# Two handoffs between layers: the last rows' statistics earlier, the last row's moments on ScalarE, row copies in one-bank tiles with guess products between them, small clears on GpSimd

## The chip, the cores and the metric

One core of one Trainium2 chip. The metric is the device time of one execution in microseconds. An execution's clock is the mean granted TensorE clock of its core, 1.000 being full speed. The ratios and their intervals are those of the record, from the fast runs of the same rounds; they are not quite the ratios of the medians that are quoted beside them, nor of the plain means (clears_only: 1586.44 over 1586.81 us is 0.9998, the record has 1.0000).

## The reference, cut to what matters

```python
x = x + A(layernorm(x))      # A: irfft2(rfft2(x) * W), 2048 tokens x 640
x = x + B(layernorm(x))      # B: attention by segments of 32 with 8 memory rows, 32 heads of 128
x = x + A(layernorm(x))
x = x + B(layernorm(x))
```

Layer B's memory goes from one segment to the next, so the kernel first guesses all memories and then repairs the guess. The first guess is made from sums over each segment ("u", made from the tile "psu") and Wv; its products are "psvb". The result of the last layer norm of A is what B starts from: u, and the transposed tokens "hT". The stretch in which A ends and B begins is called the handoff here. There are two, near 107 and 885 us.

## The kernel before

A works through 16 tiles ("rows") of 128 tokens. Row i's eviction, its moments, the inverse deviation of a pair of rows and the scaling ("norm") are spread over ScalarE, VectorE and GpSimd. This is the loop and what follows it (cut):

```python
for i in range(16 + 1):
    ...
    if i >= 5 and i % 2 == 1:
        norm((i - 5) // 2)              # VectorE, then a store
    if i >= 2:
        stats(i - 2)                    # VectorE: two BATCH_NORM_STATS2, one AGGREGATE
    ...
    if 1 <= i <= 16:
        tokens(i - 1)                   # ScalarE evicts the row: the "last token tile" is row 15
    ...
    if i >= 4 and i % 2 == 0:
        inverse((i - 4) // 2, nc.gpsimd)   # ScalarE: log and exponential; GpSimd: the scale
    ...
stats(15)
norm(6)
for s0 in range(14):
    handoff.add_u(pp, xna[:, s0, :], s0)   # TensorE: segment sums of one row, 5 products
big = handoff.big(pp)                      # one tile over two PSUM banks
inverse(7, nc.vector)
...
norm(7)
for s0 in (14, 15):
    handoff.add_u(pp, xna[:, s0, :], s0)
handoff.finish(pp)                         # ScalarE: u <- psu
...
pairs = [handoff.rows_in(pp, xna, 3, 2 * n, ps=big[:, 2 * n:2 * n + 2]) for n in range(2)]   # transposes
ones = [handoff.rows_in(pp, xna, q, 4) for q in (2, 3)]
for job, on_dve in ((pairs[0], True), (pairs[1], False), (ones[0], True), (ones[1], True)):
    handoff.do(handoff.rows_out(job, on_dve))     # row copies by VectorE or ScalarE
handoff.guess1(pp)                                # 160 products, four ScalarE evictions
```

The small clears at the start of layer B stand in VectorE's queue:

```python
nc.vector.memset(sums_sb[:, GQ:], 1.0)
for KT in KTs:
    for a, b in ((502, 512), (1007, 1024), (1519, 1536), (2035, 2048)):
        nc.vector.memset(KT[:, a:b], 0.0)
```

Of the kernel before, what the change touches and what calls it, by code (L numbers as in the profile page):

```python
# [10 lines left out]
FP32 = mybir.dt.float32  # L11
BF16 = mybir.dt.bfloat16
I32 = mybir.dt.int32
ALU = mybir.AluOpType
ACTF = mybir.ActivationFunctionType
# [4 lines left out]
S, D = 2048, 640  # L20
# [81 lines left out]
def _ln_stats(nc, st, mv, x_row, t):  # L102
    for hlf in range(2):
        nc.vector.bn_stats(out=st[:, t % 2, hlf, :], in_=x_row[:, hlf * 320:(hlf + 1) * 320])
    nc.vector.bn_aggr(out=mv[:, t, :], in_=st[:, t % 2, :, :])
# [86 lines left out]
class LayerA:  # L192
# [330 lines left out]
    def tokens(self, x_dst, xn_dst, handoff=None):  # L523
        tc, g, UT, Gd, Ti, x = self.tc, self.g, self.UT, self.Gd, self.Ti, self.x
        nc = tc.nc
        xd, xnd = r16(x_dst), r16(xn_dst)
        s5 = self.ar.get("S5", f"{self.lname}tok")
        Gs = [s5.bf(2, NF) for _ in range(3)]
        xna = s5.bf(16, D)
        wk, st, mv = g["ln"], {}, {}  # L530
        halves = lambda ap: ap.rearrange("p (a b) -> p a b", a=2)
        pp = self.pp
# [29 lines left out]
        def stats(s0):  # L562
            _ln_stats(nc, st[s0 // 2], mv[s0 // 2], x[:, s0, :], s0 % 2)

        def inverse(q, small):
            rs[q], _ = _ln_inverse(nc, wk, mv[q], 2, g["eps"], small)

        def norm(q):
            xno = xna[:, 2 * q:2 * q + 2, :]
            _ln_scale(nc, mv[q], rs[q], x[:, 2 * q:2 * q + 2, :], xno, 2)  # L570
            nc.sync.dma_start(out=xnd[:, 2 * q:2 * q + 2, :], in_=xno)

        with tc.manual_schedule(engines={nc.tensor.engine, nc.scalar.engine, nc.vector.engine}):
            moved, late = [], []
            for i in range(16 + 1):
                for f in moved:
                    f()
                moved = []
                if late:
                    late.pop(0)()  # L580
                if i >= 5 and i % 2 == 1:
                    norm((i - 5) // 2)
                if i >= 2:
                    stats(i - 2)
                if i < 16:
                    spectrum_d(i)
                if 1 <= i <= 16:
                    tokens(i - 1)
                for f in late:
                    f()  # L590
                late = []
                if i >= 4 and i % 2 == 0:
                    inverse((i - 4) // 2, nc.gpsimd)
                if handoff is None:
                    continue
                if i < 10:
                    handoff.wv_piece(i)
                if i == 5:
                    handoff.memory(pp)
                if i >= 8 and i % 4 < 3:  # L600
                    n = i % 4
                    jobs = handoff.rows_out(handoff.rows_in(pp, xna, i // 4 - 2, 2 * n), n != 1 and i < 16)
                    if n == 1:
                        late = jobs
                    else:
                        moved = jobs
            stats(15)
            norm(6)
            if handoff is not None:
                for s0 in range(14):  # L610
                    handoff.add_u(pp, xna[:, s0, :], s0)
                big = handoff.big(pp)
            inverse(7, nc.vector)
            if handoff is not None:
                handoff.do(moved)
                second = handoff.rows_in(pp, xna, 2, 2)
            norm(7)
            if handoff is not None:
                for s0 in (14, 15):
                    handoff.add_u(pp, xna[:, s0, :], s0)  # L620
                handoff.finish(pp)
                handoff.do(handoff.rows_out(second, False))
                pairs = [handoff.rows_in(pp, xna, 3, 2 * n, ps=big[:, 2 * n:2 * n + 2]) for n in range(2)]
                ones = [handoff.rows_in(pp, xna, q, 4) for q in (2, 3)]
                for job, on_dve in ((pairs[0], True), (pairs[1], False), (ones[0], True), (ones[1], True)):
                    handoff.do(handoff.rows_out(job, on_dve))
                handoff.guess1(pp)
        pp.release()


H, DH, MEM, SEG, NSEG = 32, 128, 8, 32, 64
# [37 lines left out]
class _Stream:  # L669
# [15 lines left out]
    GQ = GS * SW  # L685
# [330 lines left out]
def _b_fast_pass(tc, g, bs, env, flag_col, nxt=None):  # L1016
    nc = tc.nc
    st = bs.st
    hT, gq, oTm = bs.hT, bs.gq, bs.oTm
    ones = g["ones"]  # L1020
    oTx_d = g["oTx_d"]
    PRE, SW, GS, NG, NT, NQ, QPRE = st.PRE, st.SW, st.GS, st.NG, st.NT, st.NQ, st.QPRE
    scale = float(DH) ** -0.5
# [6 lines left out]
    last = {}  # L1030
    ar = env["ar"]
    GQ, NL = st.GQ, NQ - st.GQ * (NG - 1)
# [5 lines left out]
    accR, accS = s3.f32(GQ + NL), s3.f32(GQ + NL)  # L1038
# [5 lines left out]
    Es = [s5.bf(512) for _ in range(2)]  # L1044
    Rb1, sums_sb = s5.f32(NQ), s5.f32(GQ + NL)
    Rs = [s4.f32(GQ + NL), g["R"][:]]
    for t in (accR, accS):
        nc.gpsimd.memset(t, 0.0)
    if True:
        nc.vector.memset(sums_sb[:, GQ:], 1.0)  # L1050
        for KT in KTs:
            for a, b in ((502, 512), (1007, 1024), (1519, 1536), (2035, 2048)):
                nc.vector.memset(KT[:, a:b], 0.0)
        Vt = {}

        def load_w(hp):
# [110 lines left out]

        def sums_ln(h):
            nc.scalar.activation(out=Rs[h % 2], in_=sums_sb, func=ACTF.Ln, bias=g["floor"][:, 0:1])
            nc.gpsimd.tensor_tensor(out=accS, in0=accS, in1=sums_sb, op=ALU.add)  # L1170
            if 0 < h < H - 1:
                sums_acc(h - 1)

        def sums_acc(h):
            nc.gpsimd.tensor_tensor(out=accR, in0=accR, in1=Rs[h % 2], op=ALU.add)

        def sums_back(h):
            R = Rs[h % 2]
# [52 lines left out]
        out = _FastOut(tc, g, env, nxt)  # L1231
# [15 lines left out]
        bufs, blocks = [s3.at(0, HL, 256), s6.at(0, HL, 256)], {}  # L1247
# [9 lines left out]
        if True:  # L1257
            for h in range(H + 2):
# [35 lines left out]
                elif h == H:  # L1294
# [5 lines left out]
                    x = ar.get("S4", f"b{bs.lname}x").bf(16, D)  # L1300
# [26 lines left out]
    with octx:  # L1327
# [17 lines left out]
        n = [0]  # L1345
# [61 lines left out]
class BStart:  # L1407
# [35 lines left out]
        nc.vector.tensor_copy(out=self.hT[:, :, 0:MEM], in_=psm[:, :, 0:MEM])  # L1443
        nc.vector.tensor_copy(out=self.gq[:, :, 0:1], in_=psm[:, :, MEM - 1:MEM])

    def guess1(self, pp):
        nc = self.tc.nc
        self.s6 = self.ar.get("S6", f"b{self.lname}")
        self.vb = self.s6.at(2 * 3 * 5 * 256, H, NSEG)
        for q in range(4):  # L1450
            ps = pp.tile([128, 2, 512], FP32, name="psvb", tag="pg", bufs=3)[:, 0, :]
            for h8 in range(8):
                h = 8 * q + h8
                for c in range(5):
                    nc.tensor.matmul(ps[:, h8 * NSEG:(h8 + 1) * NSEG], lhsT=self.Wv_sb[:, c, h * 128:(h + 1) * 128], rhs=self.u[:, c, :],  # L1455
                                     start=(c == 0), stop=(c == 4))
            nc.scalar.copy(out=self.vb[:, 8 * q:8 * q + 8, :].rearrange("p a b -> p (a b)"), in_=ps)

    def big(self, pp):
        return pp.tile([128, 4, 4, 128], BF16, name="pstrb", tag="pg", bufs=3)  # L1460

    def do(self, jobs):
        for f in jobs:
# [223 lines left out]
```

## Time and profile before

| before | value | how to read it |
|---|---|---|
| time | 1587.33 us median of 3 (1586.22 to 1587.96) | one core |
| profiled execution | 1583.7 us, clock 0.998 | the trace is of one execution, not of the median one |
| last token tile to u | 6.56 us in both handoffs | start of ScalarE's eviction of row 15 to start of u |
| u to first psq | 9.00 us in handoff 1, 7.76 us in handoff 2 | row copies and guess products |

The lines of the views are in the prediction below. A timeline line gives start and length in us, engine, line of the source and operation, and in brackets the idle time before it and who ended it. Lines of the changed kernel have other numbers for the same code: L1053 became L1074, L1085 L1106, L1433 L1460, L1457 L1490, L1507 L1540.

### The profile page before, as it was taken

What the parts mean: (1) busy time and instruction counts of PE and PEld (TensorE: products, weight loads), DVE (VectorE), ACT (ScalarE), POOL (GpSimd) and SP (SyncE); (2) the same over time, 40 slices, a digit from 0 to 9 for tenths busy, and PEclk for the clock granted to TensorE, in tenths of its full rate; (3) what the DMA queues carried; (4) which work ended last, traced back from release to release, by engine and by line L of the source; (5) the groups of instructions that cost most, each with busy time, mean ns of one, the idle gap of its engine ahead of it and who ended that gap; (6) DMA issues with size and microseconds to landing.
All of it is one profiled execution on the core that took longest, in us unless ns stands there. A gap on an engine that the chain in (4) does not pass through costs nothing.

```text
span 1583.7 us, 36625 instructions
## 1 busy us (share of the span) xinstructions
PE 1542.4 (97%) x14420; PEld 1073.2 (68%) x14421; DVE 786.1 (50%) x2220; ACT 831.9 (53%) x2541; POOL 283.3 (18%) x311
## 2 busy tenths in 40 slices
PE   6989999999999999999999899999999999999998
PEld 5666666666666667677766666666766666667775
DVE  7872545555454554543377535555454545554101
ACT  4474666666666666511126656666666666663000
POOL 3620111121111212100034111121211112120000
PEclk9999999999999999999999999999999999999999
DMA  4680445535444463646114514435454454537242
GB/s 167 213 301 8 122 138 139 153 111 167 135 135 139 118 176 97 209 104 184 51 49 148 187 53 120 151 114 172 131 140 130 122 173 126 145 96 226 67 127 64
DMA packets 159922, 214.13 MB, mean 135 GB/s; under 512 B 7230, under 2 KB 133500, under 8 KB 151804
## 3 DMA queue, kind: packets, MB, share of 16 engines
q1 hardware_dynamic: 159132, 209.41, 44.5%
q8 instruction: 114, 1.87, 0.5%
q0 software_dynamic: 608, 2.30, 0.4%
q14 instruction: 68, 0.56, 0.1%
HBM read 166.59 MB, written 45.09 MB: 134 GB/s over the span
## 4 chain that ended last, share of the span: by engine, by line
PE 89%; DVE 4%; POOL 3%; issue 2%; ACT 1%; DMA 1%; SPq 0%; DVEq 0%; POOLq 0%; ACTq 0%
PE psv L1132 19%; PE psk L1066 18%; PE psx L1366 18%; PE psq L1066 17%; PE pso L1201 5%; PE pss L1142 4%; PE psl L1160 2%; PE psg L541 1%; PE psq L1085 1%; PE psm L840 1%; PE psg L1519 1%; DVE A1tmp_S L456 1%; DVE A2tmp_S L456 1%; PE psvb L1455 0%; DMA A1x_S<-in_A_x_dram 0%
## 5 line engine op out<-in xcount | busy, mean ns | idle before, releaser
L1066 PEld LDWEIGHTS <-bB_S 128*128 128x128 bf16 x3180 | 258.1, 97 | 174.7 <-issue 1.1
L1210 DVE TENSOR_TENSOR bB_S<-pso,bB_S 128x480 bf16<-128x480 f32 (+1 forms) x320 | 189.6, 593 | 246.7 <-PE pso L1201 235.6
L1145 ACT ACTIVATE bB_S<-pss 128x269 bf16<-128x269 f32 (+5 forms) x576 | 203.9, 386 | 199.2 <-PE pss L1142 194.0
L1366 PE MATMUL psx<-Wo_sb,bB_S 128*128 128x320 bf16 x2048 | 287.7, 299 | 0.0
L1125 DVE CAST bB_S<-psk 128x495 bf16<-128x495 f32 (+3 forms) x320 | 191.8, 600 | 114.1 <-PE psk L1066 75.8
L1366 PEld LDWEIGHTS <-bB_S 128*128 128x128 bf16 x2048 | 197.1, 98 | 74.3 <-DVE bB_S L1210 0.7
L1146 DVE TENSOR_TENSOR bB_S<-bB_S,maskf 128x269 bf16<-128x269 bf16 (+5 forms) x576 | 159.5, 289 | 162.1 <-ACT bB_S L1145 162.1
L1170 POOL TENSOR_TENSOR bB_S<-bB_S,bB_S 128x634 f32<-128x634 f32 x64 | 97.9, 1530 | 770.3 <-ACT bB_S L1166 770.3
L1134 ACT CAST bB_S<-psv 128x512 bf16<-128x512 f32 (+1 forms) x288 | 161.1, 560 | 75.7 <-PE psv L1132 75.0
L1110 ACT ACTIVATE bB_S<-psq 128x96 bf16<-128x96 f32 x300 | 152.4, 508 | 91.3 <-PE psq L1066 90.4
L1132 PE MATMUL psv<-bB_S,B1hT_S 128*128 128x256 bf16 x1360 | 166.2, 273 | 0.0
L1132 PE MATMUL psv<-bB_S,B2hT_S 128*128 128x256 bf16 x1360 | 166.2, 273 | 0.0
L1066 PE MATMUL psk<-B1hT_S,bB_S 128*128 128x495 bf16 (+3 forms) x800 | 162.5, 343 | 0.4 <-ACT bB_S L1087 0.2
L1066 PE MATMUL psk<-B2hT_S,bB_S 128*128 128x495 bf16 (+3 forms) x800 | 162.5, 343 | 0.3 <-ACT bB_S L1087 0.2
L1142 PEld LDWEIGHTS <-bB_S 128*128 128x128 bf16 x1216 | 99.7, 97 | 84.4
L1066 PE MATMUL psq<-B1hT_S,bB_S 128*128 128x495 bf16 (+5 forms) x780 | 153.2, 336 | 0.0
L1066 PE MATMUL psq<-B2hT_S,bB_S 128*128 128x495 bf16 (+5 forms) x780 | 153.2, 336 | 0.0
L1132 PEld LDWEIGHTS <-B2hT_S 128*128 128x128 bf16 x1360 | 127.5, 98 | 14.6 <-issue 0.2
L1132 PEld LDWEIGHTS <-B1hT_S 128*128 128x128 bf16 x1360 | 127.5, 98 | 14.6 <-issue 0.2
L1142 PE MATMUL pss<-bB_S 128*128 128x132 bf16 (+8 forms) x1216 | 133.2, 216 | 0.1
L1201 PE MATMUL pso<-bB_S,bB_S 128*128 128x132 bf16 (+8 forms) x1216 | 120.3, 216 | 1.5 <-DVE oTmf L1211 1.4
L1201 PEld LDWEIGHTS <-bB_S 128*128 128x128 bf16 x1216 | 90.7, 98 | 22.9 <-DVE oTmf L1211 4.0
(271 smaller groups left out, 1538.5 us busy)
## 6 DMA issues: line engine op xcount, KB each, us to landing
bB_S<-Rd SPq DMA_DIRECT2D x62, 1059.5 KB
oTx_d<-bB_S SPq DMA_DIRECT2D x60, 512.0 KB
bB_S<-oTx_d SPq DMA_DIRECT2D x46, 512.0 KB
bB_S<-in_B_Wq_dram SPq DMA_DIRECT2D x32, 320.0 KB
bB_S<-in_B_Wk_dram SPq DMA_DIRECT2D x32, 320.0 KB
bB_S<-in_B_Wv_dram SPq DMA_DIRECT2D x32, 320.0 KB
Wo_sb<-in_B_Wo_dram SPq DMA_DIRECT2D x4, 1280.0 KB
B1wv_S<-in_B_Wv_dram SPq DMA_DIRECT2D x10, 512.0 KB
```

The source lines that it names most:

```text
L1066: nc.tensor.matmul(ps, lhsT=w[:, ch, hh * 128:(hh + 1) * 128], rhs=src[:, ch, lo:hi], start=(ch == 0), stop=(ch == 4))
L1110: nc.scalar.mul(out=qv[:, :, 0:SEG], in_=x_view(ps, o, n)[:, :, 1:SW], mul=scale)
L1125: nc.vector.tensor_copy(out=KTs[h % 2][:, lo:hi], in_=ps[:, 0:hi - lo])
L1132: nc.tensor.matmul(ps[:, i * 256:(i + 1) * 256], lhsT=hT[:, ch, st.hcol((t + i) * 128):st.hcol((t + i) * 128) + 128], rhs=w["Wv"][:, ch, : ...
L1134: nc.scalar.copy(out=V[:, t:t + n, :].rearrange("p a b -> p (a b)"), in_=ps[:, 0:n * 256])
L1142: nc.tensor.matmul(ps[:, off - o0:off - o0 + hi - lo], lhsT=KT[:, t * 128:(t + 1) * 128], rhs=QT[:, lo:hi], start=True, stop=True)
L1145: nc.scalar.activation(out=E[:, 0:n], in_=ps[:, 0:n], func=ACTF.Exp)
L1146: nc.vector.tensor_tensor(out=P[:, o0:o0 + n], in0=E[:, 0:n], in1=bs.mask[:, o0:o0 + n], op=ALU.mult)
L1170: nc.gpsimd.tensor_tensor(out=accS, in0=accS, in1=sums_sb, op=ALU.add)
L1201: nc.tensor.matmul(pso[:, lo - q0:hi - q0], lhsT=V[:, t, (h % 2) * 128:(h % 2 + 1) * 128], rhs=P[:, off:off + hi - lo], start=(i == 0), st ...
L1210: nc.vector.tensor_tensor(out=oT.rearrange("p (r s j) -> p r s j", r=16, j=2)[:, :, s0:s0 + ns, :], in0=byclass(po), in1=rx, op=ALU.mult)
L1366: self.tc.nc.tensor.matmul(ps[:, 0:320], lhsT=lhs(h, k // 2), rhs=self.g["Wo_sb"][:, h, c0:c0 + 320], start=(h == 0), stop=(h == H - 1))
```

## The change

It shortens the two handoffs. The moments of row 15 move to ScalarE; the moments of rows 11 to 14 go ahead of the norms; the segment sums of rows 0 to 9 go ahead of the last rows' statistics; the two-bank tile becomes two one-bank tiles; the guess products are put between the transposes in five pieces; nine small clears move to GpSimd, and two large ones become copies at the first head. The core of the diff:

```diff
+        def act_stats(s0):
...
+            nc.scalar.activation(out=scr, in_=x[:, s0, :], func=ACTF.Identity, scale=-D ** -1.5, accum_out=nm[:])
+            nc.scalar.activation(out=scr, in_=x[:, s0, :], func=ACTF.Square, scale=D ** -0.5, bias=nm[:, 0:1], accum_out=m[:, 1:2])
+            nc.gpsimd.tensor_scalar_mul(out=m[:, 0:1], in0=nm[:], scalar1=-D ** 0.5)
...
+                last = i >= 13
+                if i >= 2 and last:
+                    stats(i - 2)
                 if i >= 5 and i % 2 == 1:
                     norm((i - 5) // 2)
-                if i >= 2:
+                if i >= 2 and not last:
                     stats(i - 2)
...
+                if i == 16:
+                    for s0 in range(10):
+                        handoff.add_u(pp, xna[:, s0, :], s0)
...
-            stats(15)
+            act_stats(15)
...
-                for job, on_dve in ((pairs[0], True), (pairs[1], False), (ones[0], True), (ones[1], True)):
-                    handoff.do(handoff.rows_out(job, on_dve))
-                handoff.guess1(pp)
+                pairs = [handoff.rows_in(pp, xna, 3, 2 * n, ps=handoff.big(pp)) for n in range(2)]
+                ones = [handoff.rows_in(pp, xna, 2, 4)]
+                vb = [handoff.guess1(pp, 0)]
+                ones.append(handoff.rows_in(pp, xna, 3, 4))
+                handoff.do(handoff.rows_out(pairs[0], True))
+                handoff.do(handoff.rows_out(pairs[1], False))
+                vb.append(handoff.guess1(pp, 1))
...
-        nc.vector.memset(sums_sb[:, GQ:], 1.0)
+        nc.gpsimd.memset(sums_sb[:, GQ:], 1.0)
...
-                nc.vector.memset(KT[:, a:b], 0.0)
+                nc.gpsimd.memset(KT[:, a:b], 0.0)
...
+    GUESS = ((0, 8), (8, 16), (16, 24), (24, 28), (28, 32))
...
-        return pp.tile([128, 4, 4, 128], BF16, name="pstrb", tag="pg", bufs=3)
+        return pp.tile([128, 2, 512], FP32, name="pstrb", tag="pg", bufs=3)[:, 0, :].bitcast(BF16).rearrange("p (c i k) -> p c i k", c=2, i=4)
```

More of the change, by code (lines that the diff above doesn't have):

```diff
@@ L563, in stats @@
             _ln_stats(nc, st[s0 // 2], mv[s0 // 2], x[:, s0, :], s0 % 2)
+        def act_stats(s0):
+            m, scr = mv[s0 // 2][:, s0 % 2, :], Gs[1].rearrange("p a b -> p (a b)")[:, 0:D]
+            nm = wk.tile([128, 1], FP32, name="lnnm", tag="lnnm")
+            nc.scalar.activation(out=scr, in_=x[:, s0, :], func=ACTF.Identity, scale=-D ** -1.5, accum_out=nm[:])
+            nc.scalar.activation(out=scr, in_=x[:, s0, :], func=ACTF.Square, scale=D ** -0.5, bias=nm[:, 0:1], accum_out=m[:, 1:2])
+            nc.gpsimd.tensor_scalar_mul(out=m[:, 0:1], in0=nm[:], scalar1=-D ** 0.5)
         def inverse(q, small):
@@ L606, in tokens @@
                         moved = jobs
-            stats(15)
+            act_stats(15)
             norm(6)
-            if handoff is not None:
-                for s0 in range(14):
-                    handoff.add_u(pp, xna[:, s0, :], s0)
-                big = handoff.big(pp)
             inverse(7, nc.vector)
             if handoff is not None:
+                for s0 in range(10, 14):
+                    handoff.add_u(pp, xna[:, s0, :], s0)
                 handoff.do(moved)
@@ L622, in tokens @@
                 handoff.do(handoff.rows_out(second, False))
-                pairs = [handoff.rows_in(pp, xna, 3, 2 * n, ps=big[:, 2 * n:2 * n + 2]) for n in range(2)]
-                ones = [handoff.rows_in(pp, xna, q, 4) for q in (2, 3)]
-                for job, on_dve in ((pairs[0], True), (pairs[1], False), (ones[0], True), (ones[1], True)):
-                    handoff.do(handoff.rows_out(job, on_dve))
-                handoff.guess1(pp)
+                pairs = [handoff.rows_in(pp, xna, 3, 2 * n, ps=handoff.big(pp)) for n in range(2)]
[5 more added lines that the diff above has]
+                vb.append(handoff.guess1(pp, 1))
+                handoff.do(handoff.rows_out(ones[0], True))
+                handoff.guess1_out(0, vb[0], nc.scalar.copy)
+                vb.append(handoff.guess1(pp, 2))
+                handoff.guess1_out(1, vb[1], nc.scalar.copy)
+                handoff.do(handoff.rows_out(ones[1], True))
+                vb.append(handoff.guess1(pp, 3))
+                handoff.guess1_out(2, vb[2], nc.scalar.copy)
+                vb.append(handoff.guess1(pp, 4))
+                handoff.guess1_out(3, vb[3], nc.vector.tensor_copy)
+                handoff.guess1_out(4, vb[4], nc.scalar.copy)
         pp.release()
@@ L1046, in _b_fast_pass @@
     Rs = [s4.f32(GQ + NL), g["R"][:]]
-    for t in (accR, accS):
-        nc.gpsimd.memset(t, 0.0)
     if True:
-        nc.vector.memset(sums_sb[:, GQ:], 1.0)
+        nc.gpsimd.memset(sums_sb[:, GQ:], 1.0)
         for KT in KTs:
             for a, b in ((502, 512), (1007, 1024), (1519, 1536), (2035, 2048)):
-                nc.vector.memset(KT[:, a:b], 0.0)
+                nc.gpsimd.memset(KT[:, a:b], 0.0)
         Vt = {}
@@ L1169, in sums_ln @@
             nc.scalar.activation(out=Rs[h % 2], in_=sums_sb, func=ACTF.Ln, bias=g["floor"][:, 0:1])
-            nc.gpsimd.tensor_tensor(out=accS, in0=accS, in1=sums_sb, op=ALU.add)
+            if h:
+                nc.gpsimd.tensor_tensor(out=accS, in0=accS, in1=sums_sb, op=ALU.add)
+            else:
+                nc.gpsimd.tensor_copy(out=accS, in_=sums_sb)
             if 0 < h < H - 1:
@@ L1174, in sums_acc @@
         def sums_acc(h):
-            nc.gpsimd.tensor_tensor(out=accR, in0=accR, in1=Rs[h % 2], op=ALU.add)
+            if h:
+                nc.gpsimd.tensor_tensor(out=accR, in0=accR, in1=Rs[h % 2], op=ALU.add)
+            else:
+                nc.gpsimd.tensor_copy(out=accR, in_=Rs[0])
         def sums_back(h):
@@ L1444, in memory, with guess1, guess1_out @@
         nc.vector.tensor_copy(out=self.gq[:, :, 0:1], in_=psm[:, :, MEM - 1:MEM])
-    def guess1(self, pp):
+    GUESS = ((0, 8), (8, 16), (16, 24), (24, 28), (28, 32))
+    def guess1(self, pp, q):
         nc = self.tc.nc
-        self.s6 = self.ar.get("S6", f"b{self.lname}")
-        self.vb = self.s6.at(2 * 3 * 5 * 256, H, NSEG)
-        for q in range(4):
-            ps = pp.tile([128, 2, 512], FP32, name="psvb", tag="pg", bufs=3)[:, 0, :]
-            for h8 in range(8):
-                h = 8 * q + h8
-                for c in range(5):
-                    nc.tensor.matmul(ps[:, h8 * NSEG:(h8 + 1) * NSEG], lhsT=self.Wv_sb[:, c, h * 128:(h + 1) * 128], rhs=self.u[:, c, :],
-                                     start=(c == 0), stop=(c == 4))
-            nc.scalar.copy(out=self.vb[:, 8 * q:8 * q + 8, :].rearrange("p a b -> p (a b)"), in_=ps)
+        if q == 0:
+            self.s6 = self.ar.get("S6", f"b{self.lname}")
+            self.vb = self.s6.at(2 * 3 * 5 * 256, H, NSEG)
+        ps = pp.tile([128, 2, 512], FP32, name="psvb", tag="pg", bufs=3)[:, 0, :]
+        h0, h1 = self.GUESS[q]
+        for h in range(h0, h1):
+            for c in range(5):
+                nc.tensor.matmul(ps[:, (h - h0) * NSEG:(h - h0 + 1) * NSEG], lhsT=self.Wv_sb[:, c, h * 128:(h + 1) * 128], rhs=self.u[:, c, :],
+                                 start=(c == 0), stop=(c == 4))
+        return ps
+    def guess1_out(self, q, ps, copy):
+        h0, h1 = self.GUESS[q]
+        copy(out=self.vb[:, h0:h1, :].rearrange("p a b -> p (a b)"), in_=ps[:, 0:(h1 - h0) * NSEG])
     def big(self, pp):
-        return pp.tile([128, 4, 4, 128], BF16, name="pstrb", tag="pg", bufs=3)
+        return pp.tile([128, 2, 512], FP32, name="pstrb", tag="pg", bufs=3)[:, 0, :].bitcast(BF16).rearrange("p (c i k) -> p c i k", c=2, i=4)
     def do(self, jobs):
```

## The prediction

"They" are VectorE's and ScalarE's copies, and "that pairing" is VectorE's row copies beside GpSimd's clears, for which no effect was counted. The sum: 0.85 + 2.1 + 0.85 + 0.9 = 4.7 us, to 1582.6 us.

> **What bounds the kernel now.** I read the page first, its busy times and the chain that ended last. TensorE is busy 97% of the span and carries 89% of the chain, so a change counts only where TensorE stands still.
>
> ```profile
> PE 1542.4 (97%) x14420; PEld 1073.2 (68%) x14421; DVE 786.1 (50%) x2220; ACT 831.9 (53%) x2541; POOL 283.3 (18%) x311
> ...
> PE 89%; DVE 4%; POOL 3%; issue 2%; ACT 1%; DMA 1%; SPq 0%; DVEq 0%; POOLq 0%; ACTq 0%
> ```
>
> The change touches only the end of each layer A and its handoff to layer B, of which there are two. So next came the busy times by stretch: the two handoffs (from the last token tile to the first query matmul, "psq") and the layer-B stretches behind them. The columns are the stretch, its length, then busy time and instructions of TensorE, weight loads, VectorE, ScalarE and GpSimd, the clock and the DMA share.
>
> ```profile
> 107.00:122.50 15.50, 10.81 (x284) 9.70 (x284) 9.68 (x39) 8.87 (x21) 1.00 (x5) 1.00 0.71 214
> 885.30:899.50 14.20, 10.70 (x284) 9.70 (x285) 9.59 (x39) 8.81 (x21) 1.00 (x5) 1.00 0.76 233
> 122.50:640.00 517.50, 516.83 (x4825) 349.14 (x4825) 258.07 (x762) 322.91 (x1027) 91.84 (x60) 1.00 0.44 128
> ```
>
> The third line shows TensorE idle for 0.67 us in the 517.5 us after the first handoff: whatever moves the first psq earlier moves the end by as much. The first two show the pool to win from: 4.7 us idle in handoff 1 and 3.5 us in handoff 2, 8.2 us in all, 0.5% of the run.
>
> What is waited for there is in the table of waits of each handoff (total us, times, longest). First handoff:
>
> ```profile
> DVE bB_S L1053 <- DMA xn<-A1tok_S: 2.3, 1, 2.3
> ACT B1hT_S L1487 <- DVE B1hT_S L1494: 2.1, 1, 2.1
> ...
> PE psvb L1455 <- ACT B1hT_S L1494: 1.1, 1, 1.1
> ...
> PE pstr L1472 <- ACT B1hT_S L1491: 0.9, 1, 0.9
> ...
> PE psq L1085 <- ACT bB_S L1457: 0.7, 1, 0.7
> ```
>
> Second handoff:
>
> ```profile
> PE pstr L1472 <- ACT B2hT_S L1491: 0.9, 1, 0.9
> ...
> ACT B2hT_S L1487 <- DVE B2hT_S L1494: 0.9, 1, 0.9
> ...
> PE psq L1085 <- ACT bB_S L1457: 0.7, 1, 0.7
> ```
>
> The first handoff has a chain the second lacks. VectorE's clear of K's pad columns (L1053) waits for a store to land; the row copies behind it in VectorE's queue start at 115.70; ScalarE's copies of the other half of the same PSUM tile wait for VectorE's last one (L1494); the guess products wait for ScalarE. That is why handoff 1 takes 9.4 us from the last norm (112.3 to 113.1) to psq at 122.50, and handoff 2 only 8.2 us (norm's end 891.3, psq 899.47).
>
> Three rows of the timeline (start, length) are my anchors: the last row's moments on VectorE, the last norm, and "u", after which the guess products may run.
>
> ```profile
> 109.75 0.83 DVE L104 BATCH_NORM_STATS2 lnst<-A1x_S 128x6 f32<-128x320 bf16 x2
> ...
> 112.29 0.80 DVE L127 TENSOR_SCALAR A1tok_S<-A1x_S,lnmv,lnrs 128x640 bf16<-128x640 bf16 x2
> ...
> 113.50 0.44 ACT L1507 ACTIVATE u<-psu 128x320 bf16<-128x320 f32 x1 [0.53 <-PE psu L1433]
> ```
>
> The moments on ScalarE cost what the same two operations cost in the cold start (timeline, ScalarE):
>
> ```profile
> 4.62 0.74 ACT L283 ACTIVATE A1xn_S<-A1x_S 128x640 bf16<-128x640 bf16 x1 [2.59 <-DMA A1x_S<-in_A_x_dram]
> 5.27 0.19 ACT L283 ACTIVATION_READ_ACCUMULATOR A1xn_S<-A1x_S 128x1 f32 x1
> 5.49 0.83 ACT L284 ACTIVATE A1xn_S<-A1x_S,A1xn_S 128x640 bf16<-128x640 bf16 x1
> 6.22 0.19 ACT L284 ACTIVATION_READ_ACCUMULATOR A1xn_S<-A1x_S,A1xn_S 128x1 f32 x1
> ```
>
> From 4.62 to 6.41 is 1.79 us for a row; VectorE's own way is 1.1 us (two halves 0.83, aggregate 0.21, gaps).
>
> [...] the trace agrees that they are ordered (2.1 us and 0.9 us above), although the two halves of this tile are a bank each: the order is kept by the tile. Two one-bank tiles take it away. [...] No run so far shows that pairing. I count none.
>
> **The change part by part** (times of handoff 1; the program orders of both builds were compared, the waits taken from the built instructions).
>
> 1. Reordered statistics, last row on ScalarE. In the old order VectorE does norm(5), three rows' statistics, norm(6), then the scale of pair 7 and norm(7) at 112.29. New: VectorE is free at 106.25 (it idled 0.76 us before norm(5)), so row 13's statistics run 106.25 to 107.35, norm(5) to 108.1, row 14's to 109.2. ScalarE is free at 107.63 and takes pair 6's logarithm and exponential (0.52) to 108.2, the moments of row 15 (1.8) to 110.0, pair 7's logarithm and exponential to 110.6. GpSimd finishes pair 6's scale 1.18 us after its exponential, at 109.4, so norm(6) runs 109.4 to 110.2, beside ScalarE. Four small VectorE operations (0.80 as now) put norm(7) at 111.4 to 111.5. **Gain 0.85 us in each handoff.** ScalarE now sets it, not VectorE; GpSimd's product for the mean (0.2) lies beside it. Dropping GpSimd's two 0.6 us clears takes 0.2 us off pair 5's scale, which is hidden, as row 13's statistics now end later. "u" moves from 113.50 to 112.65.
>
> 2. Single banks, interleaved guess products, clears gone. Counted from the start of "u": ScalarE's u and copies of the second pair take 1.95 (113.50 to 115.45), then with no wait for VectorE its row-12-to-15 copies 1.72 (117.56 to 119.28 now), to 3.67. VectorE starts its copies as soon as the first eight transposes are done (0.45), takes 1.75, to 2.2, and is never in the way again. TensorE: sixteen transposes and four more until 1.1, then the first 40 guess products (31 ns each, 1.25) to 2.35 while ScalarE still copies, where it now stands still 0.9 us; four transposes to 2.6; 40 more to 3.85 (their bank freed by VectorE at 2.2); 40 more, freed by ScalarE at 3.7, to 5.05; 20 to 5.65; 20 to 6.3. ScalarE's evictions (0.57 each) begin at 3.7, 4.25 and 5.25, in time for the banks. The last is half as long (0.4) and starts 0.2 after the last product: 6.9. The first psq still waits for that one, as its wait shows. Now it is 9.00 (113.50 to 122.50) and 7.76 (891.71 to 899.47). **Gain 2.1 us in handoff 1, 0.9 us in handoff 2.** It differs since only handoff 1 has the 2.3 us store wait.
>
> 3. The sums' clears become copies at the first head: GpSimd only, off the path. Zero.
>
> 4. The last two xn stores now stand ahead of the first Wk and Wv loads in the DMA queue's order: Wk is issued some 2 us later (110.3 instead of 108.68) and Wv some 3 us. The first K matmul is at 137.14. Hidden; zero.
>
> Sum: 0.85 + 2.1 + 0.85 + 0.9 = 4.7 us, so 1587.3 - 4.7 = **1582.6 us**.
>
> **The rivals.** (a) ScalarE becomes the bound: it now carries moments, a pair of copies and four evictions in one queue. If its copies run late by 1 us in each handoff, two thirds of the gain of part 2 go: 1585. For it: by my count TensorE waits for ScalarE by a hair at the third group. Against: ScalarE is busy 8.87 us of 15.5 now and loses its 2.1 us wait. (b) The store wait only moves: ScalarE's first write of Q needs the same store. Then handoff 1 keeps its 2.1: 1584.7. Against: the store lands at 115.4, that write comes after 119. (c) Late Wk or Wv loads, with the DMA busy 71 to 76% there: a new wait up to 3 us, 1585. Against: over 20 us of slack. (d) The gain is larger, if the first psq no longer waits for the last eviction (0.6 us in each): 1581.4. The built wait speaks against it.
>
> **Range and chances.** Even all of the idle TensorE time in both handoffs, 8.2 us, is 0.5%, so 2% faster is out of reach; 2% slower would need 32 us from parts that are a few us long. Rivals (a) to (c) pull to 1585, (d) to 1581.4; the runs before spread over 1.7 us. Range 1580.5 to 1585.3; faster 0.01, within 2% 0.98, slower 0.01.
>
> **What would show it.** Right: "u" about 0.85 us earlier against the last token tile; no VectorE wait for a store; no wait of ScalarE's row copies for VectorE; no TensorE wait for the row-copy bank in front of the last transposes; both handoffs equally long, about 6.9 us from u to psq; TensorE idle after that unchanged. Wrong: a ScalarE operation that TensorE waits for over 1 us in the guess products, moments well over 1.8 us, a wait at the first K or V matmuls, or handoffs that still differ.

## The result, and the profile after

The changed kernel took **1580.66 us** in the median of 4 (1580.17 to 1581.50); before took 1587.44 us in the same rounds. The ratio is 0.9959, with an interval from 0.9942 to 0.9976: some 6.5 us less. The result is 1.9 us under the predicted 1582.6 and inside the range, 0.2 us from its lower end.

The two traces, split at the same four events, give this account (us; "span" is the profiled execution):

| | start to last token tile 1 | tile to u | u to psq | psq to tile 2 | tile to u | u to psq | psq to end | span |
|---|---|---|---|---|---|---|---|---|
| before | 106.94 | 6.56 | 9.00 | 762.65 | 6.56 | 7.76 | 684.20 | 1583.7 |
| after | 107.74 | 5.52 | 6.60 | 762.61 | 5.52 | 6.59 | 684.31 | 1578.9 |
| after minus before | +0.80 | -1.04 | -2.40 | -0.04 | -1.04 | -1.17 | +0.11 | -4.8 |

So the handoffs won 5.65 us, and 0.8 us of it was lost again before the first of them, in code that the change doesn't touch (more of that below). First the busy times of the page of the changed kernel:

```profile
PE 1542.9 (98%) x14420; PEld 1074.0 (68%) x14421; DVE 784.2 (50%) x2198; ACT 835.6 (53%) x2549; POOL 280.3 (18%) x327
```

TensorE does the same number of instructions as before; 22 instructions have left VectorE. The same stretches as in the prediction (columns as there), the two handoffs up to the first psq and then layer B; the first one begins at 107.00 as there, which is 0.74 us ahead of this trace's last token tile:

```profile
107.00:119.86 12.86, 11.12 (x289) 10.09 (x289) 8.80 (x29) 10.73 (x26) 2.34 (x17) 1.00 0.93 278
882.48:894.59 12.11, 10.36 (x286) 9.69 (x284) 8.05 (x27) 10.19 (x25) 1.95 (x15) 1.00 0.88 268
119.86:637.36 517.50, 516.81 (x4826) 349.14 (x4826) 258.15 (x762) 323.34 (x1027) 90.28 (x60) 1.00 0.45 128
```

TensorE's idle time in a handoff fell from 4.7 and 3.5 us to 1.7 us in each. Behind it, TensorE idles 0.69 us in 517.5 us, where it was 0.67: no part of the gain is given back in layer B. The table of waits of the first handoff:

```profile
POOL bB_S L1074 <- DMA xn<-A1tok_S: 3.6, 1, 3.6
...
DVE bB_S L1490 <- PE psvb L1484: 1.6, 1, 1.6
PE psu L1460 <- DVE A1tok_S L127: 1.2, 2, 0.8
ACT bB_S L1490 <- PE psvb L1484: 1.0, 2, 0.6
...
PE psq L1106 <- ACT bB_S L1490: 0.5, 1, 0.5
```

The wait of the clears for the store (2.3 us on VectorE before) is now 3.6 us on GpSimd, where nobody waits for it. The wait of ScalarE for VectorE's row copies (2.1 us) and TensorE's wait in front of the last transposes (0.9 us) are not in the table any more. The evictions now wait for TensorE, and not the other way round. The timeline of the first handoff:

```profile
108.77 0.72 ACT L568 ACTIVATE A1tok_S<-A1x_S 128x640 bf16<-128x640 bf16 x1
109.40 0.19 ACT L568 ACTIVATION_READ_ACCUMULATOR A1tok_S<-A1x_S 128x1 f32 x1
109.68 0.83 ACT L569 ACTIVATE A1tok_S<-A1x_S,lnnm 128x640 bf16<-128x640 bf16 x1
...
110.42 0.19 ACT L569 ACTIVATION_READ_ACCUMULATOR A1tok_S<-A1x_S,lnnm 128x1 f32 x1
...
112.05 0.80 DVE L127 TENSOR_SCALAR A1tok_S<-A1x_S,lnmv,lnrs 128x640 bf16<-128x640 bf16 x2
...
113.26 0.44 ACT L1540 ACTIVATE u<-psu 128x320 bf16<-128x320 f32 x1 [0.54 <-PE psu L1460]
...
113.78 1.39 DVE L1520 COPY B1hT_S<-pstrb 128x480 bf16<-128x480 bf16 x2 [0.93 <-ACT u L1540]
113.96 0.43 POOL L1074 MEMSET bB_S<- 128x10 bf16 x8 [3.60 <-DMA xn<-A1tok_S]
...
115.61 3.79 PE L1484 MATMUL psvb<-u,B1wv_S 128*128 128x64 bf16 x120
...
119.86 2.45 PE L1106 MATMUL psq<-B1hT_S,bB_S 128*128 128x480 bf16 x11 [0.46 <-ACT bB_S L1490]
```

The moments on ScalarE take 108.77 to 110.61. The last 120 guess products run without a wait in a single piece. VectorE's two row copies take 1.39 us beside GpSimd's clears, which overlap 0.43 us of them, and took 1.39 us without them before (from 115.70). So in these two traces the clears did not stretch the copies, and the prediction had counted nothing for it.

### The profile page after: what moved, and what is told of

Read it like the earlier page. It is cut to its first block, busy times and chain, and to the rows that moved or that the text cites. A ratio compares the mean times of both kernels' runs of the same rounds, so it can differ in the third digit from the quotient of the medians.

```text
span 1578.9 us, 36639 instructions
## 1 busy us (share of the span) xinstructions
PE 1542.9 (98%) x14420; PEld 1074.0 (68%) x14421; DVE 784.2 (50%) x2198; ACT 835.6 (53%) x2549; POOL 280.3 (18%) x327
## 5 line engine op out<-in xcount | busy, mean ns | idle before, releaser
L1153 PEld LDWEIGHTS <-B2hT_S 128*128 128x128 bf16 x1360 | 127.5, 98 | 14.6 <-issue 0.2
L1153 PEld LDWEIGHTS <-B1hT_S 128*128 128x128 bf16 x1360 | 127.5, 98 | 14.6 <-issue 0.2
```

What stands on the lines that cost most here:

```text
L1153: nc.tensor.matmul(ps[:, i * 256:(i + 1) * 256], lhsT=hT[:, ch, st.hcol((t + i) * 128):st.hcol((t + i) * 128) + 128], rhs=w["Wv"][:, ch, : ...
```

## The experiments

Twelve further runs were made, two of them repeats without an edit, each with five rounds. The half-widths of the intervals are 0.0014, or 2.2 us, so times alone do not part versions that lie 2 us apart; the stretches of the traces do. In the table, H1 and H2 are the two handoffs (last token tile to first psq), "half clock" says in which of them the trace has a stretch with a granted clock of 0.50, and the clocks are those of all executions of the run (four for the first row of after, five for the others; those of the first row of before are not on record).

| kernel | median us | ratio to before (95%) | H1 | H2 | half clock in | clocks |
|---|---|---|---|---|---|---|
| before, first trace | 1587.33 | | 15.6 | 14.3 | neither | |
| before_again | 1587.41 | 1.0000 (0.9986 to 1.0014) | 15.2 | 15.1 | both | 0.995 to 0.998 |
| clears_only | 1586.68 | 1.0000 (0.9986 to 1.0014) | 14.3 | 15.0 | H2 | 0.994 to 0.998 |
| stats_only | 1583.91 | 0.9986 (0.9972 to 1.0000) | 14.6 | 13.3 | H1 | 0.996, 0.997 |
| handoff_only | 1585.85 | 0.9996 (0.9982 to 1.0009) | 14.6 | 14.6 | both | 0.995, 0.996 |
| after, first trace | 1580.66 | 0.9959 (0.9942 to 0.9976) | 12.1 | 12.1 | neither | 0.996 to 0.998 |
| after_again | 1581.78 | 0.9968 (0.9954 to 0.9982) | 12.1 | 12.1 | neither | all 0.997 |
| after_clears_back | 1580.40 | 0.9961 (0.9948 to 0.9975) | 12.4 | 12.1 | neither | 0.996 to 0.999 |
| after_stats_back | 1584.29 | 0.9986 (0.9973 to 1.0000) | 14.3 | 12.9 | H1 | 0.995, 0.996 |
| after_handoff_back | 1582.64 | 0.9978 (0.9964 to 0.9991) | 13.3 | 13.3 | neither | 0.997, 0.998 |
| before_warm | 1587.84 | 1.0017 (1.0003 to 1.0031) | 14.8 | 15.1 | neither | 0.996 to 0.998 |
| after_row15_dve | 1582.61 | 0.9974 (0.9961 to 0.9988) | 12.3 | 12.3 | neither | 0.996, 0.997 |
| after_no_reorder | 1586.46 | 0.9996 (0.9982 to 1.0009) | 14.7 | 14.7 | both | 0.995, 0.996 |
| after_more | 1583.12 | 0.9978 (0.9964 to 0.9992) | 13.2 | 13.2 | neither | 0.996 to 0.998 |

### The kernel before, once more

No edit. It measures what a trace of the same kernel differs by.

> The kernel before, unchanged, for a second trace of it. In the first trace handoff 1 took 15.56 us from the last token tile's eviction (start) to the first psq, handoff 2 14.32 us; the kernel after takes 12.12 and 12.11 us. The two profiled runs differ by 4.7 us, the medians by 6.8 us. My theory: what is left over is the wait of VectorE's clear for the store of x, whose landing time is not the same in every execution, so here handoff 1 or 2 should be longer than in the first trace (up to 2 us), and the total near 1587.4. Rival: the handoffs are the same to 0.1 us in both traces (15.56, 14.32), and the difference comes from the cold start or from elsewhere.

The time was the same, but the trace was not: handoff 2 took 15.1 us in place of 14.3, and the store wait in front of the clears in handoff 1 was 1.3 us in place of 2.3. So the expected cause, a later store, is not what made handoff 2 longer. The windows (columns as above; the last but two is the granted clock) of the stretch that begins with the last transposes, here and in the first trace of before:

```profile
892.40:895.81 3.41, 3.41 (x45) 3.29 (x43) 1.63 (x10) 1.92 (x4) 0.00 (x0) 0.51 0.99 311
```

```profile
891.50:894.91 3.41, 2.49 (x63) 2.37 (x61) 2.40 (x13) 2.31 (x5) 0.00 (x0) 1.00 0.93 299
```

In one execution TensorE was granted half its clock for 3.41 us, and was busy all of that time; in the other it was at full speed, did more (63 instructions in place of 45) and even idled. The tile's own line (least, median and largest duration in ns) shows what it does to one product:

```profile
L1472 PE MATMUL pstrb<-ident,A2tok_S x16: 220/314/314, 892.4 to 893.9; 128*128 128x128 bf16 x16
```

In the first trace all sixteen took 219 or 220 ns. So **before has executions with and without a half-clock stretch in the handoff**, and the prediction had been worked out from one without. Scanned in steps of 0.1 us, the half-clock stretches of the traces (but for those at the very end) are 3.4 us long, and 6.8 us in one place of after_more. The two in the handoffs of this trace begin at 114.2 and 892.4 us, and in the 3.41 us before them TensorE was busy for 2.06 and 2.05 us. In the first trace it was busy for as little as 1.99 us in 3.41 us (from 112.10 us) and stayed at full clock. The end of the spectrum (A's transform), code that the change leaves alone, differs between executions too. The same stretch of before and of after (us from the start, columns as above):

```profile
69.00:72.50 3.50, 1.82 (x12) 1.14 (x12) 3.50 (x5) 1.84 (x6) 2.42 (x6) 1.00 1.07 362
72.50:75.90 3.40, 2.49 (x20) 1.98 (x21) 2.39 (x4) 2.11 (x8) 0.56 (x1) 1.00 0.63 214
```

```profile
69.00:72.50 3.50, 1.82 (x12) 1.14 (x12) 3.50 (x5) 1.84 (x6) 2.43 (x6) 1.00 1.07 362
72.50:75.90 3.40, 2.79 (x13) 1.98 (x14) 2.38 (x4) 1.47 (x5) 0.56 (x1) 0.50 0.64 216
```

TensorE was busy for the same 1.82 us ahead of it, and yet one execution fell to half clock and the other did not. This goes with the 0.8 us that the changed kernel's trace lost before the first handoff: the four traces without a stretch here (before, handoff_only, before_warm, after_row15_dve) reach the last token tile at 106.8 to 107.3 us, as do the two in which it began at 71.6 and 71.8 us (clears_only, stats_only); the eight in which it began at 72.3 us or later reach it at 107.7 to 109.2 us.

The handoffs of all fourteen traces show the same. Nine of them have a half-clock stretch, and in the 3.41 us before it TensorE was busy for between 1.34 us (after_stats_back, handoff 1) and 2.06 us (before_again, handoff 1). In handoff 2 of after_stats_back it was busy for 1.34 us, too, in the 3.41 us from 887.80 us, and stayed at full clock. So the same hole may or may not cost the clock; on what that depends was not shown. Nor need the two handoffs of one execution be independent draws: of the six traces with such a stretch in a handoff, three have it in both.

### One part alone: the clears

```diff
-        nc.vector.memset(sums_sb[:, GQ:], 1.0)
+        nc.gpsimd.memset(sums_sb[:, GQ:], 1.0)
-                nc.vector.memset(KT[:, a:b], 0.0)
+                nc.gpsimd.memset(KT[:, a:b], 0.0)
```

> The kernel before with only the clears of K's pad columns and of the sums' tail moved from VectorE to GpSimd. My theory: VectorE no longer waits for the store, so handoff 1 becomes as long as handoff 2: 15.56 to 14.3 us; handoff 2 loses at most the 0.3 us of the clears; ScalarE's wait for VectorE's copies of the shared tile stays (0.6 to 0.9 us). Total 1.2 to 1.6 us less than before by the trace, more if the store is late in most executions (up to 3 us by the clock). Rival: the store wait only moves to ScalarE's first write of Q: handoff 1 stays at 15.5.

The clears' waits for the store are now GpSimd's, and u to psq of handoff 1 is 7.8 us, which was 9.0 in the first trace of before and 8.6 in the second: the store wait was real, and the clears removed it. Yet the time did not move (ratio 1.0000). This trace has a half-clock stretch in handoff 2 (8.4 us from u to psq in place of 7.8), so what the store wait had cost is within what the executions differ by anyway. The expected 1.2 to 1.6 us were not seen.

### One part alone: the statistics

```diff
+                last = i >= 13
+                if i >= 2 and last:
+                    stats(i - 2)
                 if i >= 5 and i % 2 == 1:
                     norm((i - 5) // 2)
-                if i >= 2:
+                if i >= 2 and not last:
                     stats(i - 2)
...
-            stats(15)
+            act_stats(15)
```

> The kernel before with only the reordered statistics and the last row's moments on ScalarE. My theory: u starts 1.0 us earlier after the last token tile's eviction (5.5 instead of 6.56 us) in both handoffs; in handoff 2 the first psq follows (14.32 to 13.3 us); in handoff 1 VectorE still waits for the store, so nearly nothing is left at psq (15.56 to 15.2 or more). Total 1.0 to 1.4 us less. Rival: both handoffs gain 1.0, total 2.0 less.

By the ratio it is worth some 2.2 us, more than any other part alone, though the interval reaches 1. In handoff 2, at full clock, the stretch from the last token tile to u fell from 6.6 to 5.5 us and u to psq stayed at 7.8. In handoff 1 a half-clock stretch began near 109.4 us, in the middle of it, and took that gain away (6.8 us to u); VectorE's clears did not wait for the store in this trace, so u to psq was 7.8 us there too and not the 9.0 that the expectation had kept. The hole ahead of that stretch is partly this build's own: TensorE was busy for 1.51 us there at its least (the 3.41 us from 105.40 us), where in after_handoff_back, which has the same statistics, it was busy for 2.14 us at its least (from 105.80 us).

### One part alone: the banks, the order of transposes and guess products

```diff
+                if i == 16:
+                    for s0 in range(10):
+                        handoff.add_u(pp, xna[:, s0, :], s0)
...
+                pairs = [handoff.rows_in(pp, xna, 3, 2 * n, ps=handoff.big(pp)) for n in range(2)]
...
+                vb = [handoff.guess1(pp, 0)]
```

(and the rest of the change's edits of the guess products and of the tile, without the clears and the statistics)

> The kernel before with only the handoff's part: one-bank tiles, guess products between the transposes, five evictions; clears stay on VectorE, statistics as before. My theory: handoff 2 goes from u to psq in 6.7 instead of 7.76 us (VectorE's 0.27 us of clears are hidden); in handoff 1 the second group of products waits for VectorE's copy, which waits for the store: 8.4 instead of 9.00. Total 1.5 to 1.8 us less. Rival (all of the gain of the handoff is in this part): 2.4 us less in handoff 1 too, total 3.5 less.

The ratio is 0.9996: nothing that the runs can tell from zero, where the same edits shorten u to psq by 2.4 and 1.2 us in the changed kernel. The trace shows why. Both handoffs are at half clock from about u on, and u to psq takes 7.9 and 8.0 us where the changed kernel at full clock takes 6.6. The waits of its second handoff name the cause; the second line is the same wait in the first trace of before:

```profile
PE psu L1446 <- DVE A2tok_S L127: 2.2, 2, 1.8
```

```profile
PE psu L1433 <- DVE A2tok_S L127: 1.3, 2, 0.8
```

The segment sums of rows 0 to 9 were moved ahead, and with the old order of statistics TensorE has nothing left to do while it waits for the norm of rows 12 and 13. In the 3.41 us before the drops it was busy for 1.43 and 1.93 us (109.59 to 113.00 and 887.89 to 891.30 us). **The hole that the one part of the change makes deeper is the hole that the other part fills.**

### The changed kernel once more, and with each part put back

No edit for the first; the other three put one of the three parts above back as it was.

> The kernel after, unchanged: a second trace and a comparison on another chip. Theory: the gain is the handoffs' own work (5.5 us from the last eviction to u, 6.6 us from u to the first psq, in both handoffs, 12.1 us each) and, beside it, fewer stretches in which TensorE runs at half clock in the handoffs: the kernel before had two of them there in its second trace and none in its first. So both handoffs again 12.1 us and at full clock; time 5.5 to 7 us less than before. Rival: the absence of half-clock stretches in the handoffs of the first trace was luck; then one or both handoffs are up to 1 us longer here with a clock of 0.5 in them, and the gain is nearer 5.

The ratio was 0.9968, after 0.9959 in the first rounds, with handoffs of 12.1 us each. It repeats; the 5.1 us by the ratio lie a little under the expected 5.5 to 7.

> The kernel after, with K's and the sums' clears back on VectorE. Theory: the second group of guess products waits for VectorE's row copy, that for the clears, those for the store of x in handoff 1: u to psq 6.6 to 8.2 us there, by when the store lands; handoff 2 within 0.3 us of 6.6. Total 0.3 to 2 us more than after. Rival: with one-bank tiles VectorE has slack, so both stay at 6.6 and the total does not change.

With the clears back on VectorE nothing is lost (0.9961 against 0.9968 on the same chip). VectorE waits 1.1 us for the store in handoff 1, and u to psq is 6.9 us in place of 6.6: TensorE has other products to do in the meantime.

> The kernel after, with the old order of the statistics and the last row's moments on VectorE. Theory: last eviction to u is 6.56 instead of 5.5 us in both handoffs, u to psq stays at 6.6 where the clock is full: 2.1 us more than after. Rival: TensorE stands still longer before u, so it falls to half clock in the handoffs more often: 6.6 becomes 7.5 to 8 with a clock of 0.5 in the stretch, and the total is 3 to 4 us more.

Without the statistics part the time is 3.0 us up on the same chip (means 1584.25 and 1581.29 us). In the traces 1.8 us of it are the stretch to u (6.46 and 6.34 us, against 5.51 in both). The rest goes with the clock, as the rival had it: the trace has a half-clock stretch in handoff 1 (u to psq 7.8 us, but 6.6 in handoff 2, which has none), and four of its five executions have a clock of 0.996 and one 0.995, where all five of after_again have 0.997.

> The kernel after, with the old handoff (one shared two-bank tile, all transposes before the guess products, four evictions). Theory: last eviction to u stays 5.5 us, u to psq 7.7 us at full clock in both handoffs (ScalarE's copies wait for VectorE's 0.8 us; transposes wait 0.9 us for their bank): 2.2 us more than after. Rival: with half-clock stretches 8.4 us: 3 to 4 us more.

Without the banks and the new order of products the time is 1.5 us up (1582.80 and 1581.29 us); u to psq is 7.8 us in both handoffs. Both stay at full clock in its trace. Its handoffs are 2.4 us longer in all than those of after_again, but its trace has no half-clock stretch near 850 us, in code that the change leaves alone, and takes 761.75 us from the first psq to the second last token tile, after_again 762.85. Four of its five executions have a clock of 0.998, where after_again has 0.997. So 1.5 us is rather less than this part is worth at an equal clock.

### The new order of statistics without the moments on ScalarE, and the reverse

```diff
-            act_stats(15)
+            stats(15)
```

> The changed kernel with the last row's moments back on VectorE; the new order of statistics and norms stays. Theory: the new order brings most of the 1.04 us, since pair 6's statistics no longer stand behind a norm; then the stretch from the last token tile to u is 5.8 to 6.0 us in both handoffs (5.5 in the changed kernel, 6.5 before) and the time is 0.4 to 1 us above the changed kernel's. Rival: the moments on ScalarE bring all of it; then the stretch is back at 6.5 us and the time 2 us up.

Last token tile to u took 5.7 us in both handoffs, a little under what was expected. So of the 1.04 us a handoff the moments on ScalarE bring 0.17, and the new order 0.87. In time it lies 4.1 us under before by the ratio, where after_again lay 5.1 under; the intervals do not part the two.

```diff
-                last = i >= 13
-                if i >= 2 and last:
-                    stats(i - 2)
                 if i >= 5 and i % 2 == 1:
                     norm((i - 5) // 2)
-                if i >= 2 and not last:
+                if i >= 2:
                     stats(i - 2)
```

> The other half: the changed kernel with the last row's moments on ScalarE, but statistics behind the norms as before. Theory (the new order brings most): the stretch to u is 6.0 to 6.4 us, since pair 6's logarithm and exponential, and with them the moments, start some 0.7 us later on ScalarE; time 1 to 2 us above the changed kernel's. Rival (moments bring all): 5.5 us and the changed kernel's time.

This missed on both counts. The stretch to u was 6.7 us in both handoffs, 0.1 us longer than before: the moments on ScalarE alone bring nothing. And **the whole gain of the change was gone**: ratio 0.9996, its fastest execution (1585.49 us) slower than the slowest of after_row15_dve in the same rounds (1583.18 us). The timeline of ScalarE, pair 6's logarithm and the start of the moments, in this kernel (its last token tile starts at 108.87):

```profile
110.63 0.29 ACT L112 ACTIVATE lnnb<-lnmv,eps 128x2 f32<-128x2 f32 x1 [1.07 <-DVE lnmv L105]
...
111.07 0.72 ACT L568 ACTIVATE A1tok_S<-A1x_S 128x640 bf16<-128x640 bf16 x1
```

ScalarE waits for row 13's statistics, which stand behind a norm on VectorE; the moments then start 2.20 us after the last token tile, in the changed kernel 1.03 us after it (108.77 less 107.74). Then TensorE stands in the deeper hole (at its worst, busy for 1.08 us in 3.41 us), and the clock falls in both handoffs. The window of the second, and that of the changed kernel's from its last transposes:

```profile
893.80:897.21 3.41, 3.41 (x54) 3.41 (x52) 2.44 (x7) 3.32 (x9) 0.02 (x1) 0.50 1.05 309
```

```profile
887.80:891.21 3.41, 3.41 (x99) 3.35 (x97) 2.62 (x8) 3.18 (x6) 0.41 (x8) 1.00 0.81 242
```

54 products in 3.41 us at half clock, 99 at full clock, with TensorE busy throughout in both. u to psq took 8.0 us in both. The two handoffs together are 5.2 us longer than in after_again (29.4 and 24.2 us), and so is the mean time (1586.46 and 1581.29 us, from two sets of rounds in which before itself had means of 1586.63 and 1586.35 us). Here the account closes: 1.2 us a handoff before u, and 1.4 us a handoff of half clock behind it. It closes on the means only: the two profiled executions are 7.1 us apart, and the other 1.9 us lie outside the handoffs (the one of after_no_reorder is the slowest of its five).

### Filling TensorE's waits in the kernel before

```diff
+    def warm(self, xrow, n):
+        for k in range(n):
+            self.tc.nc.tensor.matmul(self.idle[:, k % 8 * NSEG:(k % 8 + 1) * NSEG], lhsT=xrow[:, 0:128], rhs=self.g["sel2"][:], start=True, stop=True)
```

> The kernel before with 34 idle products in each handoff, in TensorE's waits ahead of the last rows' sums, into a PSUM bank that nothing reads. They compute nothing that is used and take no wait away. Theory: part of the time before is TensorE's half clock in the handoffs, [...] filled up, the handoffs stay at full clock in every execution. Then every execution has a mean clock of 0.997 or more, the trace shows no half-clock stretch in either handoff, handoff 2 stays at 14.3 us, and the mean is about 0.8 us (0.05%) under the kernel before's, near 1585.8 us. Rival: the clock falls for another reason; then about half of the executions still have a clock of 0.995 or 0.996, and the time is the kernel before's or a little longer for the added products.

The products stand ahead of the sums of row 12 (22) and of rows 14 and 15 (12). In the trace the clock did what the theory said: no half-clock stretch in either handoff, with at least 2.25 us busy in any 3.41 us up to u and 2.13 us in the stalls ahead of psq. But not every execution has the expected clock of 0.997: two have 0.996. And the time did not fall: 1587.84 us, by the interval of the ratio 0.0003 to 0.0031 more than before. One part of it the trace shows, in the second handoff:

```profile
893.67 4.83 PE L1464 MATMUL psvb<-u,B2wv_S 128*128 128x64 bf16 x159
899.11 0.19 PE L1464 MATMUL psvb<-u,B2wv_S 128*128 128x64 bf16 x1 [0.61 <-issue]
...
899.97 0.37 PE L1088 MATMUL psq<-B2hT_S,bB_S 128*128 128x480 bf16 x1 [0.67 <-ACT bB_S L1466]
```

TensorE stood still for 0.61 us ahead of the very last guess product, for nothing that the profile shows ("issue"), and 0.29 us at the same place in handoff 1. Before has no such wait there. So u to psq was 8.5 us where it is 7.8 without the wait, and the full clock won nothing. Those two executions, at 1590.31 and 1591.75 us, are longer still, and they were not profiled: why they are is open. As a test of the clock this run shows only that, in the one traced execution, both handoffs stayed at full clock with more work in the hole; that this saves time in the kernel before, it does not show.

### A version meant to be faster

```diff
+                first = handoff.big(pp)
+                ones = [handoff.rows_in(pp, xna, 2, 4, ps=handoff.big(pp, 1))]
...
-    GUESS = ((0, 8), (8, 16), (16, 24), (24, 28), (28, 32))
+    GUESS = ((0, 8), (8, 16), (16, 24), (24, 30), (30, 32))
```

(all transposes ahead of the guess products, and a smaller last piece)

> A version meant to beat the changed kernel: four transposes move ahead of the last norm, all others ahead of the guess products, and the last piece of the guess products has 2 heads in place of 4. Expected: u to the first query product 6.2 us in place of 6.6, from a shorter last eviction and fewer transposes behind u; together at most 1 us, 0.05%, which the interval will hardly part from nothing. If it is slower, the third group of transposes sits in a bank that now comes free later, and a wait of TensorE ahead of the guess products shows it.

It was slower than the changed kernel: ratio 0.9978, u to psq 7.7 us in both handoffs in place of 6.6. The wait is the one that the expectation named for that event:

```profile
118.37 3.66 PE L1485 MATMUL psvb<-u,B1wv_S 128*128 128x64 bf16 x120 [1.38 <-ACT B1hT_S L1530]
```

TensorE waits 1.38 us until ScalarE's row copies free a bank, which is the wait that the change's interleaving avoids. No version tried beats the changed kernel.

## Why the prediction was right, and what it left out

**Step 1, statistics: 0.85 us a handoff predicted, 1.04 measured.** The moments took 1.84 us (1.8 predicted). Counted from the last token tile, the last norm began 0.2 us sooner than the working had it (4.31 us against 111.45 less 106.94). The working priced the new order and ScalarE's moments together; the runs part them. The order alone brings 0.87 us, and the moments 0.17 in its presence and nothing without it, although the working had ScalarE set the end.

**Step 2, banks and interleaving: 2.1 and 0.9 predicted, 2.40 and 1.17 measured.** u to psq was predicted at 6.9 us in both handoffs and is 6.6. By the timeline the last products ended 6.14 us after u (6.3 in the working), and the last eviction followed them by 0.04 us and not 0.2. The difference between the handoffs was read rightly in that one trace, but it is no constant: the store wait was 2.3 us in it and 1.3 us in the next. With TensorE at half clock both handoffs of before took 8.5 to 8.6 us from u to psq.

**Steps 3 and 4: zero predicted.** The order of the weight loads costs nothing that shows: TensorE's idle time behind handoff 1 is 0.69 us, 0.67 before. The clears of the sums have no experiment of their own. The sums hold to 0.1 us, except that rival (a) comes to 1584.6 and not 1585, and a wait of the full 3 us in (c) to 1585.6, outside the range.

**What was left out: TensorE's clock.** The prediction took the traced handoffs, at full clock, for all executions. In 32 executions of the kernel before (27 that three sets of rounds were compared with, and the five of before_again), 16 have a clock of 0.997 or more and a mean of 1585.91 us, and 16 one of 0.996 or less and a mean of 1587.36 us. (One half-clock stretch lowers the mean clock by half of 3.41 us in 1584 us, about 0.001. The split is rough: in the traces of before and after half clock also begins after TensorE's work is done, and some 3.3 and 4.5 us of it lie inside the span. With those and two stretches of 3.4 us, near 72.5 and 847.2 us, the traced execution of after reads 0.996, both handoffs at full clock.) All 32 have a mean of 1586.64 us. Nine executions of the changed kernel have a mean of 1581.05 us. So against the executions of before with the higher clock the change wins 4.9 us, and against the mean of all 5.6 us, as it also keeps the clock up in the handoffs (no half clock there in either of its two traces). That 4.9 is so near the predicted 4.7 is partly luck: in the traces, both at full clock there, the handoffs won 5.65 us, more than the steps' sum, and 0.8 us was lost ahead of the first. It is luck, too, that the result stayed in the range: rival (d), which set its lower end, fell, and the clock was not among the rivals. The first rounds showed 6.5 us, whose interval holds both. That the clock makes this last difference is shown for after_no_reorder, by its traces and times together; for before it is a correlation, and the direct test (before_warm) brought a new wait and did not settle it.

With the old order of statistics, 8 of 12 traced handoffs have a half-clock stretch (before_warm, where the hole is filled, not counted); with the new order, 1 of 14. By traces that is 5 of 6 and 1 of 7. One more look at the traces speaks against luck. Let a stretch of 3.41 us slide over a handoff, from the last token tile to the first psq; these are the places where TensorE is busy least, in the first handoff of before, handoff_only and after:

```profile
112.10:115.51 3.41, 1.99 (x35) 1.58 (x33) 1.03 (x6) 2.76 (x6) 0.00 (x0) 1.00 0.83 272
```

```profile
109.22:112.63 3.41, 1.11 (x20) 0.81 (x19) 3.20 (x13) 1.89 (x6) 0.78 (x4) 1.00 1.03 309
```

```profile
109.50:112.91 3.41, 2.12 (x42) 1.60 (x39) 2.49 (x10) 2.99 (x8) 0.62 (x3) 1.00 1.04 355
```

In both handoffs of its two traces the changed kernel never goes below 2.12 us, and each of the nine half-clock stretches came after 2.06 us or less. That this is why it kept the clock, and that it would in every execution, is the author's estimate from these traces. Before, at 1.99 us, lies in the range that went both ways (1.34 to 2.06 us); so do after_row15_dve (1.95 us) and after_handoff_back (1.92 us), which may lose the clock in other executions.

**The rivals.** (a) fell: the guess products wait for no ScalarE operation. (b) fell: the store wait moved to GpSimd, off the path. (c) fell, as step 4 says. (d) fell too: psq still waits for the last eviction, 0.46 us.

## What to carry to other kernels

Read a short TensorE stretch in more than one trace before pricing it, with the granted clock beside the busy time: in after_no_reorder a hole that cost 1.2 us a handoff by itself came with 1.4 us more just behind it, at half clock. When work is moved ahead out of a wait, ask what is left to fill the wait; two edits that look separate may only pay together, and undoing each of them alone is what shows it. In a queue in program order, where a statistic stands against a norm can be worth more than the engine that it runs on (here 0.87 and 0.17 us a handoff).
